# Seven block products in three accumulator banks instead of four

## The chip, the cores and the metric

The kernel runs on one core of one Trainium2 chip. The metric is the device time of one execution in microseconds (us). Before the change it is 582.73 us, the median of three runs (582.6 to 583.14).

## What is computed

A banded attention (two batches, eight heads, 768 positions of 64 numbers) is followed by two feed-forward blocks. The change touches the second one alone:

```python
def _moe2_ref(x, w_in, w_out):
    h = x @ w_in                                            # 1536 x 512 by 512 x 2048
    g = np.maximum(h, 0.0) + np.log1p(np.exp(-np.abs(h)))   # softplus
    return (g @ w_out).astype(np.float32)
```

Inputs are float32. The kernel keeps float32 accuracy by splitting each operand in a high and a low part, and making three matmuls of each product (`mm3`, lines 167 to 169).

## The kernel before

The last stage (`stage4`) computes this second block. It goes over three blocks t of 512 tokens, and in each over 16 slices f of 128 hidden columns. A slice is a bank `h` of 128 hidden columns by 512 tokens, made by 12 matmuls of 512 columns; ScalarE (ACT) and VectorE (DVE) turn it into softplus, split in `gh` and `gl`; and 12 more matmuls (`outs`) multiply these with the output weights, into four banks (`ox` and `o`, 128 tokens by 512 each) that stay open over all 16 slices. TensorE makes the `outs` of one slice while ACT and DVE work on the next.

Five pairs of slices (p = 2, 4, 6 in block 1, and p = 3, 5 in block 2) are made another way, by the function `seven`. The two slices of a pair, 256 hidden columns by 512 tokens, are seen as 2 x 2 blocks, as are the weights and the tokens, and are made of seven products of blocks instead of eight (the Strassen-Winograd scheme). The function `product` makes one block product: six matmuls of 256 columns, into one half (256 of 512 columns) of an accumulator bank. The sums of weights (`ws`, from `wr`) and of tokens (`ts`) that this needs are made by DVE and ACT ahead of the pair; the products are put together by DVE (`combine`, line 759) into `he` and `ho`, the two halves of the buffer `hp`, from which softplus goes on as for any other slice.

The banks of `h` and of the pairs come from one ring of four banks (tag "S"). A new buffer takes the bank of the one four places before it, and is written when that one's readers are done. In `seven` the four banks A, Bk, C and E are this whole ring:

- A, first half: product 1, copied out by ACT as `p1`; product 6 is later added to it.
- Bk, both halves: products 2 and 3.
- C, first half: product 4, then read once by DVE, for the sum `u3`.
- E, first half: product 5, which DVE adds to `u3`; product 7 is later added to it.

In this text the products have the numbers of the order in which they are made. Between them stand the `outs` of the slices before, written out by hand: three matmuls between products 3 and 4, nine between 5 and 6, three between 6 and 7, and nine behind 7. Blocks 1 and 2 are under a manual schedule: each engine runs its instructions in the order of the program. Waits between engines are set by the framework, which goes by tiles in accumulator memory.

Of the kernel before, what the change touches and what calls it, by code (L numbers as in the profile page):

```python
# [9 lines left out]
F32 = mybir.dt.float32  # L10
# [6 lines left out]
ALU = mybir.AluOpType  # L17
# [3 lines left out]
P = 128  # L21
B, H, S, D = 2, 8, 768, 64
# [17 lines left out]
CH = 512  # L40
NCH = NT // CH
HN, HM = slice(0, CH // 2), slice(CH // 2, CH)
# [17 lines left out]
    C=(-143.56, -520.69, 38.35, -348.75, -150.48, -361.46), T=(85.26, 85.11, 83.1, 84.82, 88.43, 82.09),  # L60
    P=(-697.11, -455.77, -631.6, -474.64, -647.58, -395.71), PV=(97.88, 94.31, 94.22, 97.88, 97.88, 169.98),
# [81 lines left out]
class Net:  # L143
# [581 lines left out]
    def stage4(self, pool, psum):  # L725
# [3 lines left out]
        def outs(t, f, g, parts=range(CH // P)):  # L729
            if f == 0:  # L730
                acc[t] = [psum.tile([P, CH], F32, tag=f"X{i}", name=f"ox{t}_{i}", bufs=1) for i in range(2)]
                acc[t] += [psum.tile([P, CH], F32, tag="PT", name=f"o{t}_{i}", bufs=2) for i in range(2)]
            wh, wl = self.w4[f]
            for i in parts:
                k = slice(i * P, (i + 1) * P)
                self.mm3(acc[t][i], (g[0][:, k], g[1][:, k]), (wh[:, 1, :], wl[:, 1, :]), f == 0, f == NF2 - 1)
# [21 lines left out]
        def combine(out, x, y, op):  # L758
            nc.vector.tensor_tensor(out=out, in0=x, in1=y, op=op)
# [49 lines left out]
        def product(ps, a, b, start=True):  # L809
            for c in range(2):  # L810
                self.mm3(ps, a(c), b(c), start and c == 0, c == 1, skip_group_check=True)

        def seven(t, p, before, todo):
            odd, even, x = self.w4[2 * p + 1], self.w4[2 * p], self.x2[t]

            def part(pair, c0):
                return lambda c: tuple(w[:, 0, (c0 + c) * P : (c0 + c + 1) * P] for w in pair)

            def tok(c0, cols):
                return lambda c: tuple(x[c0 + c][:, j, cols] for j in range(2))  # L820

            def wsum(j, c0):
                return lambda c: tuple(self.ws[j][:, k, (c0 + c) * P : (c0 + c + 1) * P] for k in range(2))

            def tsum(j, cols):
                return lambda c: tuple(self.ts[c, j][:, k, cols] for k in range(2))

            def quarter(tag, n):
                return self.dec.tile([P, CH // 2], F32, tag=tag, name=f"{n}_{t}_{p}", bufs=2)

            A, Bk, C, E = [psum.tile([P, CH], F32, tag="S", name=f"q{t}_{p}_{j}", bufs=4) for j in range(4)]
            h = self.slot(SLOT_X + 2, f"hp{t}_{p}", F32)
            he, ho = h[:, 0, :], h[:, 1, :]
            product(A[:, HN], part(odd, 0), tok(0, HN))
            p1 = quarter("dt", "p1")
            nc.scalar.copy(p1, A[:, HN])
            product(Bk[:, HN], part(even, 2), tsum(1, HN))
            product(Bk[:, HM], wsum(0, 0), tsum(1, HM))
            u2 = quarter("dc", "u2")
            combine(u2, Bk[:, HM], p1, ALU.add)  # L840
            outs(*todo[0], parts=[0])
            product(C[:, HN], wsum(1, 0), tsum(0, HM))
            u3 = quarter("dt", "u3")
            combine(u3, C[:, HN], u2, ALU.add)
            combine(he[:, HN], u3, Bk[:, HN], ALU.subtract)
            product(E[:, HN], wsum(1, 2), tsum(0, HN))
            combine(he[:, HM], E[:, HN], u3, ALU.add)
            before()
            outs(*todo[0], parts=[1, 2, 3])
            product(A[:, HN], part(odd, 2), tok(2, HN), False)  # L850
            outs(*todo[1], parts=[0])
            product(E[:, HN], wsum(0, 2), tok(2, HM), False)
            outs(*todo[1], parts=[1, 2, 3])
            e = self.softplus(pool, he, 2 * p, t)
            next(e)
            next(e)
            nc.scalar.copy(ho[:, HN], A[:, HN])
            combine(ho[:, HM], E[:, HN], u2, ALU.add)
            g = next(e)
            o = self.softplus(pool, ho, 2 * p + 1, t)  # L860
            next(o)
            next(steps.get((t, 2 * p + 1), (iter(lambda: 0, 1), ()))[0])
            next(o)
            return [(t, 2 * p, g)], (t, 2 * p + 1, o)
# [17 lines left out]
        for t in range(NCH):  # L882
            pairs = lots.get(t, ())
            with tc.manual_schedule() if t else contextlib.nullcontext():
                for f in range(NF2):
# [4 lines left out]
                    if f // 2 in pairs:  # L890
                        if f % 2 == 0:
                            def before():
                                todo.append((*last[:2], next(last[2])))

                            todo, last = seven(t, f // 2, before, todo)
                        continue
# [222 lines left out]
```

## Time and profile before

| | us |
|---|---|
| median of three runs | 582.73 |
| the profiled execution | 585.09 |
| its span, first to last instruction | 583.2 |
| TensorE busy | 573.7 |
| VectorE busy | 470.5 |
| ScalarE busy | 394.0 |

The profiled execution is 1.9 us longer than its span and 2.4 us longer than the median. In the tables of the profile PE is TensorE's matmuls, PEld its loads of weights (which run beside the matmuls before them), and the name behind "<-" in a wait is what ended it. A matmul's duration in these tables is longer than the distance to the next: they are pipelined, and the distance is what counts.

### The profile page before, as it was taken

The numbers are of one execution on the slowest core, as the hardware profiler recorded it, in microseconds if no ns is written. First come the engines' busy times: TensorE is split into PE (matmuls) and PEld (weight loads), VectorE is DVE, ScalarE is ACT, GpSimd is POOL, SyncE is SP. The second block draws the span as 40 slices with busy tenths as digits, with TensorE's granted clock in tenths as the row PEclk, the third lists the DMA queues.
The fourth block names the chain that finished last, engine by engine and source line by source line (L and its number), as shares of the span: only waits on it lengthen the run. The fifth ranks groups of instructions, "written<-read, shape, count | busy, mean of one in ns | idle before, by whom it ended". The sixth has DMA issues, their size and how long they took to land.

```text
span 583.2 us, 10109 instructions
## 1 busy us (share of the span) xinstructions
PE 573.7 (98%) x3808; PEld 476.0 (82%) x3808; DVE 470.5 (81%) x1004; ACT 394.0 (68%) x790; POOL 46.6 (8%) x113
## 2 busy tenths in 40 slices
PE   9999999999999999999999999999999999999995
PEld 7887788888788788888888788888888888888884
DVE  6889899999889976776998899965877867877663
ACT  6999967676566664554667989666665766666662
POOL 3757710000000000000000000000000000000000
PEclk9999999999999999999999999999999999999999
DMA  7666644444443632441744131000200000100002
GB/s 252 193 199 216 185 146 145 144 143 147 145 144 111 179 110 72 145 144 38 201 130 138 31 115 37 0 1 0 74 0 1 1 0 1 72 1 1 1 1 78
DMA packets 15514, 54.53 MB, mean 94 GB/s; under 512 B 1888, under 2 KB 1888, under 8 KB 15456
## 3 DMA queue, kind: packets, MB, share of 16 engines
q1 hardware_dynamic: 15312, 53.53, 30.0%
q8 instruction: 32, 0.52, 0.4%
q10 hardware_dynamic: 144, 0.26, 0.1%
q14 instruction: 26, 0.21, 0.1%
HBM read 50.64 MB, written 3.15 MB: 92 GB/s over the span
## 4 chain that ended last, share of the span: by engine, by line
PE 56%; DVE 9%; ACT 5%; DMA 4%; issue 1%; ACTq 0%; SPq 0%; DVEq 0%
PE h L168 5%; PE h L169 5%; PE h L167 5%; PE x2p L169 4%; PE x2p L167 4%; PE x2p L168 4%; PE ox L167 3%; PE ox L169 3%; PE o L168 3%; PE o L167 3%; PE o L169 3%; PE ox L168 3%; DMA raw_w<-w3t 3%; PE ab L169 3%; PE ab L167 3%; PE ab L168 3%
## 5 line engine op out<-in xcount | busy, mean ns | idle before, releaser
L194 ACT ACTIVATE dt_w<-raw_w 128x512 bf16<-128x512 bf16 x64 | 42.5, 670 | 53.5 <-DMA raw_w<-w4d 14.7
L167 PE MATMUL ab<-x,u_w 128*128 128x512 f32 x192 | 75.0, 391 | 0.3 <-ACT u_w L227 0.3
L169 PE MATMUL ab<-x,u_w 128*128 128x512 f32 x192 | 74.9, 390 | 0.3 <-DVE u_w L152 0.3
L168 PE MATMUL ab<-x,u_w 128*128 128x512 f32 x192 | 74.7, 389 | 0.0
L167 PE MATMUL h<-y,w4h 128*128 128x512 f32 x152 | 59.1, 389 | 0.0
L168 PE MATMUL h<-y,w4h 128*128 128x512 f32 x152 | 59.1, 389 | 0.0
L169 PE MATMUL h<-y,w4l 128*128 128x512 f32 x152 | 59.1, 389 | 0.0
L712 DVE SCALAR_TENSOR_TENSOR spu<-spu,spa 128x512 f32<-128x512 f32 (+1 forms) x49 | 33.2, 677 | 27.1 <-ACT spl L710 27.1
L202 DVE SCALAR_TENSOR_TENSOR dc_w<-raw_w,dt_w 128x512 uint16<-128x512 uint16 x64 | 44.2, 698 | 10.1 <-ACT dt_w L197 9.2
L721 ACT CAST gh<-spl 128x512 fp32r<-128x512 f32 x47 | 28.8, 614 | 29.9 <-DVE spl L718 29.9
L152 DVE TENSOR_TENSOR gl<-spl,gh 128x512 fp32r<-128x512 f32 x47 | 32.3, 688 | 19.6 <-ACT gh L721 19.4
L705 ACT ACTIVATE spa<-h 128x512 f32<-128x512 f32 (+1 forms) x39 | 22.8, 583 | 36.5 <-PE h L169 36.5
L197 ACT ACTIVATE dt_w<-dt_w,rebias 128x512 uint16<-128x512 uint16 x64 | 45.8, 722 | 1.3
L394 ACT ACTIVATE e<-e,st 128x196 f32<-128x196 f32 (+1 forms) x96 | 42.2, 447 | 1.5 <-DVE st L387 1.3
L169 PEld LDWEIGHTS ab<-x,u_w 128*128 128x128 f32 x192 | 36.0, 188 | 8.6 <-DVE u_w L152 1.2
L167 PEld LDWEIGHTS ab<-x,u_w 128*128 128x128 f32 x192 | 36.0, 188 | 8.4 <-ACT u_w L227 1.0
L168 PEld LDWEIGHTS ab<-x,u_w 128*128 128x128 f32 x192 | 36.0, 188 | 7.5
L408 POOL TENSOR_SCALAR e<-e,st 128x196 f32<-128x196 f32 (+1 forms) x96 | 39.7, 438 | 24.1 <-ACT e L394 16.9
L167 PE MATMUL x2p<-ab,w 128*128 128x512 f32 x96 | 37.3, 389 | 0.0
L168 PE MATMUL x2p<-ab,w 128*128 128x512 f32 x96 | 37.3, 389 | 0.0
L169 PE MATMUL x2p<-ab,w 128*128 128x512 f32 x96 | 37.3, 389 | 0.0
L167 PE MATMUL ox<-w4h,gh 128*128 128x512 f32 x94 | 37.0, 394 | 0.0
(172 smaller groups left out, 1449.6 us busy)
## 6 DMA issues: line engine op xcount, KB each, us to landing
raw_w<-w4d SPq DMA_DIRECT2D x32, 511.8 KB, 3.9
raw_w<-w SPq DMA_DIRECT2D x16, 511.8 KB, 4.7
raw_w<-w3t SPq DMA_DIRECT2D x16, 511.8 KB, 3.8
qk<-qk SPq DMA_DIRECT2D x7, 792.0 KB, 4.7
raw_wo<-wod SPq DMA_DIRECT2D x8, 511.8 KB, 3.7
v<-vu SPq DMA_DIRECT2D x8, 400.0 KB, 5.8
v<-v SPq DMA_DIRECT2D x8, 384.0 KB, 4.8
out<-os SPq DMA_DIRECT2D x11, 256.0 KB, 2.5
```

The costliest lines, as they stand in the source:

```text
L152: return engine.tensor_tensor(out=lo, in0=x, in1=hi.bitcast(F32), op=ALU.subtract)
L167: nc.tensor.matmul(ps, lhs[0], rhs[0], start=start, stop=False, **kw)
L168: nc.tensor.matmul(ps, lhs[0], rhs[1], start=False, stop=False, **kw)
L169: nc.tensor.matmul(ps, lhs[1], rhs[0], start=False, stop=stop, **kw)
L194: return nc.scalar.activation(t.bitcast(BF), x["top"].bitcast(BF), AF.Abs)
L197: return nc.scalar.activation(x["t"], x["t"], AF.Relu, bias=self.rebias[:, 0:1], scale=8.0)
L202: nc.vector.scalar_tensor_tensor(out=c, in0=x["top"], scalar=0x8000, in1=t, op0=ALU.bitwise_and, op1=ALU.bitwise_or)
L394: nc.scalar.activation(e, e, AF.Exp, bias=st[:, 0, i : i + 1], scale=-1.0, accum_out=st[:, 1, i : i + 1])
L408: nc.gpsimd.tensor_scalar(out=e, in0=e, scalar1=buf("st", h)[:, 2, i : i + 1], scalar2=1.0, op0=ALU.mult, op1=ALU.mult)
L705: nc.scalar.activation(a[:, c], ps[:, c], AF.Abs)
L712: nc.vector.scalar_tensor_tensor(out=u[:, c], in0=u[:, c], scalar=1.0, in1=a[:, c], op0=ALU.subtract, op1=ALU.subtract)
L721: self.last_hi = nc.scalar.copy(gh[:, c], l[:, c])
```

## The change

Bank E is gone. Products 5 and 7 are put into the second half of C, so that a pair takes three banks of the ring. The order of the instructions stays as it was on every engine.

```diff
-            A, Bk, C, E = [psum.tile([P, CH], F32, tag="S", name=f"q{t}_{p}_{j}", bufs=4) for j in range(4)]
+            A, Bk, C = [psum.tile([P, CH], F32, tag="S", name=f"q{t}_{p}_{j}", bufs=4) for j in range(3)]
...
             u3 = quarter("dt", "u3")
             combine(u3, C[:, HN], u2, ALU.add)
             combine(he[:, HN], u3, Bk[:, HN], ALU.subtract)
-            product(E[:, HN], wsum(1, 2), tsum(0, HN))
-            combine(he[:, HM], E[:, HN], u3, ALU.add)
+            product(C[:, HM], wsum(1, 2), tsum(0, HN))
+            combine(he[:, HM], C[:, HM], u3, ALU.add)
...
-            product(E[:, HN], wsum(0, 2), tok(2, HM), False)
+            product(C[:, HM], wsum(0, 2), tok(2, HM), False)
...
-            combine(ho[:, HM], E[:, HN], u2, ALU.add)
+            combine(ho[:, HM], C[:, HM], u2, ALU.add)
```

TensorE's rows at the end of product 4 and the start of product 5 in the first pair (block 1, p = 2), before the change. The buffers `q1_2_0` to `q1_2_3` are A, Bk, C and E; `ws` and `ts` are sums of weights and of tokens.

```order
L167 MATMUL q1_2_2_4682<-ts1_0_0_4378,ws1_2_1_4657 128x256
...
L169 MATMUL q1_2_2_4682<-ts1_1_0_4511,ws1_2_1_4657 128x256
L167 MATMUL q1_2_3_4683<-ts1_0_0_4378,ws1_2_1_4657 128x256 [waits DVE_49]
L168 MATMUL q1_2_3_4683<-ts1_0_0_4378,ws1_2_1_4657 128x256
...
L169 MATMUL q1_2_3_4683<-ts1_1_0_4511,ws1_2_1_4657 128x256
L167 MATMUL ox1_1_4616<-w4h2_3337,gh1_2_4604 128x512
```

The same place after the change.

```order
L167 MATMUL q1_2_2_4682<-ts1_0_0_4378,ws1_2_1_4657 128x256
...
L169 MATMUL q1_2_2_4682<-ts1_1_0_4511,ws1_2_1_4657 128x256
L167 MATMUL q1_2_2_4682<-ts1_0_0_4378,ws1_2_1_4657 128x256 [waits DVE_49]
L168 MATMUL q1_2_2_4682<-ts1_0_0_4378,ws1_2_1_4657 128x256
...
L169 MATMUL q1_2_2_4682<-ts1_1_0_4511,ws1_2_1_4657 128x256
L167 MATMUL ox1_1_4616<-w4h2_3337,gh1_2_4604 128x512
```

Nothing moved, and a wait for DVE stands at the same matmul; the buffer written is now that of product 4.

DVE's rows at this place after the change (before, the last of them read `q1_2_3`).

```order
L715 SCALAR_TENSOR_TENSOR spu1_3_4649<-h1_3_4631,spu1_3_4649 128x512 [waits DVE_49]
L718 TENSOR_TENSOR spl1_3_4650<-spl1_3_4650,spu1_3_4649 128x512 [waits DVE_49]
L759 TENSOR_TENSOR u2_1_2_4704<-q1_2_1_4681,p1_1_2_4690 128x256 [waits PE_49,Activation_49]
L759 TENSOR_TENSOR u3_1_2_4715<-q1_2_2_4682,u2_1_2_4704 128x256 [waits DVE_49,PE_49]
L759 TENSOR_TENSOR hp1_2_4683<-u3_1_2_4715,q1_2_1_4681 128x256 [waits DVE_49]
L759 TENSOR_TENSOR hp1_2_4683<-q1_2_2_4682,u3_1_2_4715 128x256 [waits PE_49]
```

DVE's order is that of before too. Its first reader of C is `u3`, in the fourth row.

## Rows read from the trace of the kernel before

**Rows 1.** Page, part 1: busy time of each engine.

```profile
PE 573.7 (98%) x3808; PEld 476.0 (82%) x3808; DVE 470.5 (81%) x1004; ACT 394.0 (68%) x790; POOL 46.6 (8%) x113
```

**Rows 2.** Busy time by stretch: length, busy us (instructions) by engine, clock, DMA.

```profile
419.00:570.00 151.00, 150.89 (x760) 128.17 (x759) 111.12 (x190) 99.09 (x173) 0.00 (x0) 1.00 0.02 8
```

**Rows 3.** Waits of PEld, 415 to 560 us: sum, times, longest.

```profile
PEld q L167 <- DVE spu L715: 0.7, 3, 0.3
```

**Rows 4.** Timeline, first pair, PE: last `h` matmul, then product 5.

```profile
416.98 0.39 PE L169 MATMUL h<-y,w4l 128*128 128x512 f32 x1
...
423.48 0.28 PE L167 MATMUL q<-ts,ws 128*128 128x256 f32 x1
423.60 0.28 PE L168 MATMUL q<-ts,ws 128*128 128x256 f32 x1
...
424.08 0.28 PE L169 MATMUL q<-ts,ws 128*128 128x256 f32 x1
```

**Rows 5.** Timeline, first pair, DVE: `u3`, and the sum with product 5.

```profile
424.35 0.42 DVE L759 TENSOR_TENSOR u<-q,u 128x256 f32<-128x256 f32 x1
...
425.15 0.42 DVE L759 TENSOR_TENSOR hp<-q,u 128x256 f32<-128x256 f32 x1
```

**Rows 6.** One tile (`u`): `u3` in all pairs, ns min/median/max, first and last start.

```profile
L759 DVE TENSOR_TENSOR u<-q,u x5: 425/425/425, 424.3 to 543.9; 128x256 f32<-128x256 f32 x5
```

**Rows 7.** Timeline, second pair: last `h` matmul, L715, product 5, `u3`.

```profile
438.39 0.39 PE L169 MATMUL h<-y,w4l 128*128 128x512 f32 x1
...
444.31 0.69 DVE L715 SCALAR_TENSOR_TENSOR spu<-h,spu 128x512 f32<-128x512 f32 x1
...
445.05 0.19 PEld L167 LDWEIGHTS q<-ts,ws 128*128 128x128 f32 x1 [0.20 <-DVE spu L715]
...
445.06 0.39 PE L167 MATMUL q<-ts,ws 128*128 128x256 f32 x1
...
445.28 0.28 PE L168 MATMUL q<-ts,ws 128*128 128x256 f32 x1
...
446.17 0.42 DVE L759 TENSOR_TENSOR u<-q,u 128x256 f32<-128x256 f32 x1
```

**Rows 8.** Timeline, pairs 3 to 5: last `h` matmul, product 5's second matmul, `u3`.

```profile
460.06 0.39 PE L169 MATMUL h<-y,w4l 128*128 128x512 f32 x1
...
467.09 0.28 PE L168 MATMUL q<-ts,ws 128*128 128x256 f32 x1
...
467.98 0.42 DVE L759 TENSOR_TENSOR u<-q,u 128x256 f32<-128x256 f32 x1
...
514.70 0.39 PE L169 MATMUL h<-y,w4l 128*128 128x512 f32 x1
...
521.32 0.28 PE L168 MATMUL q<-ts,ws 128*128 128x256 f32 x1
...
522.07 0.42 DVE L759 TENSOR_TENSOR u<-q,u 128x256 f32<-128x256 f32 x1
...
536.11 0.39 PE L169 MATMUL h<-y,w4l 128*128 128x512 f32 x1
...
543.00 0.28 PE L168 MATMUL q<-ts,ws 128*128 128x256 f32 x1
...
543.89 0.42 DVE L759 TENSOR_TENSOR u<-q,u 128x256 f32<-128x256 f32 x1
```

**Rows 9.** Waits of ACT, 415 to 560 us: sum, times, longest.

```profile
ACT ws L774 <- DVE wr L759: 1.0, 3, 0.4
```

**Rows 10.** The end: last matmul, and the clock after it (as in rows 2).

```profile
576.97 0.39 PE L169 MATMUL o<-w4h,glast 128*128 128x512 f32 x1
...
580.00:581.00 1.00, 0.00 (x0) 0.00 (x0) 0.00 (x0) 0.00 (x0) 0.00 (x0) 0.72 0.13 39
581.00:582.00 1.00, 0.00 (x0) 0.00 (x0) 0.00 (x0) 0.00 (x0) 0.00 (x0) 0.50 0.03 10
```

## The prediction

> **What bounds the kernel now.** The page's first part comes first: TensorE is busy for 573.7 us, 98% of the span, VectorE for 81% and ScalarE for 68% [rows 1]. Over the whole stretch that holds the five pairs the table by stretches gives TensorE 150.89 of 151.00 us at the full granted clock [rows 2]. So TensorE sets the time there, and no slice waits for anything. Whatever holds TensorE up in a pair goes to the end one for one, since no later idle time could take it in; work moved on VectorE or ScalarE costs nothing as long as TensorE doesn't wait for it. The waits of TensorE come next, and they are few: in this stretch product 5 waited three times for line 715 of VectorE, 0.7 us in all [rows 3]. That line is the last reader of `h` in the slice before the pair, and E takes that slice's bank. Last comes the order of times within a pair: when TensorE reaches product 5, and when VectorE makes `u3`.
>
> **What the change removes.** The wait for line 715. It bit in pairs 2, 3 and 5. Its price is read from the distance between the slice's last matmul and the second matmul of product 5 (the second, because a stalled first matmul has its own distance to the next): 423.60 - 416.98 = 6.62 us in pair 1 [rows 4], 445.28 - 438.39 = 6.89 in pair 2 [rows 7], and by the same reading 7.03, 6.62 and 6.89 in pairs 3, 4 and 5 [rows 8]. 6.62 is the distance without a stall, so the stalls cost 0.27, 0.41 and 0.27, in sum 0.95 us.
>
> Instructions removed: none. Matmuls, sums and copies are the same in number, size and order on each engine, and no DMA moves, so SP's and POOL's queues are as before. Those terms are zero, and nothing has to hide them.
>
> **What it adds.** The first matmul of product 5 now writes C, and it still carries a wait for VectorE. What VectorE has to do with C before this point is `u3`, which reads product 4 from the other half of the bank. A wait for that reader is the only one that the new place calls for: C's own place in the ring was freed by the slice two before the pair. So product 5, which stood right behind product 4, now stands behind product 4 and `u3`. Nothing lies between them on TensorE, and behind product 5 are queued the nine `outs` matmuls, product 6 and all the rest.
>
> When would `u3` be done? In pair 1 it starts at 424.35 [rows 5] and takes 0.425 us in every pair [rows 6], so it ends at 424.775, while TensorE begins product 5 at 423.48 [rows 4]. VectorE is not kept by TensorE here: `u3` follows `u2`, which follows the softplus of the slice before. Its times come from that slice's last matmul, through ScalarE and VectorE: 424.35 - 416.98 = 7.37 us in pair 1, 446.17 - 438.39 = 7.78 in pair 2 [rows 7], then 7.92, 7.37 and 7.78 [rows 8].
>
> How long from VectorE's end to TensorE in full flow? That is shown by the wait of today, which has the same form: line 715 ends at 444.31 + 0.69 = 445.00, the load of weights starts at 445.05 and the second matmul at 445.28 [rows 7]. So 0.28 us.
>
> In each pair the second matmul of product 5 would then be at (distance to `u3`) + 0.425 + 0.28 behind the slice's last matmul:
>
> - with the distances to `u3` as they are: 8.075, 8.485, 8.625, 8.075, 8.485; less today's 6.62, 6.89, 7.03, 6.62, 6.89 this is 1.455 + 1.595 + 1.595 + 1.455 + 1.595 = 7.70 us;
> - with 7.37 in every pair: 5 x 8.075 - 34.05 = 6.33 us.
>
> **Which of the two.** Pairs 2, 3 and 5 follow closely on another pair, and their extra 0.41, 0.55 and 0.41 us before `u3` have a visible source: ScalarE, ready to cast `ws`, waited for VectorE's sums `wr`, three times and 1.0 us in all [rows 9]. VectorE was behind with work left from the pair before. After the change TensorE is later by 1.455 us from pair 1 on, and so is the slice from which pair 2's times are counted. VectorE's leftover work is later by less. Its sum with product 5 ran at 425.15 [rows 5]; now product 5's last matmul starts at 424.08 + 1.455 and ends 0.28 later [rows 4], at 425.82, so this sum and what follows are some 0.67 us later. Against TensorE, VectorE and ScalarE thus gain about 0.79 us between the pairs (part of which ScalarE loses again, as it then waits for the next slice). The extra 0.41 to 0.55 should be gone. I take the second sum: **+6.3 us**. The distance of 7.37 can't shrink further by a lead, since it is work that starts only at the slice's last matmul, as pairs 1 and 4 show, which came after slices without leftovers.
>
> What is late next: the softplus of `he`, by 0.67 us, against a TensorE that is later by 1.455; so its `outs` don't wait. The slices after the pair take older banks than before, and carry no wait that they did not have.
>
> **A rule weighed.** In rows 7 the load of weights for the waiting matmul doesn't start before the wait ends, and the two matmuls are 0.22 us apart, where they are 0.12 apart in full flow [rows 4]; this is in the 0.28 above. The Trainium skill (TensorE: Matmul & The Clock Gate, the step on LDWEIGHTS in Part 2) says that TensorE's queue pulls a load of weights ahead of matmuls in flight. By that the load would be done during the wait. The restart would be 0.05 + 0.12 = 0.17 instead of 0.28, and the sum 5 x 7.965 - 34.05 = 5.78 us. The row has the load held back too, so I go by the row.
>
> **The sum.** 585.09 + 6.33 = 591.4 us against the profiled execution. That one lies 2.36 us above the median, so the median goes from 582.73 to **589.0 us**, 1.1% slower.
>
> **Rivals.**
>
> 1. *No lead.* VectorE stays as far behind in pairs 2, 3 and 5 as today: +7.70, 590.4 us. For it: the leftovers are longest there. Against it: the 0.79 us worked out above. 15%.
> 2. *Weights loaded during the wait.* +5.78, 588.5 us. For it: loads run ahead of matmuls everywhere else in the trace. Against: rows 7. 5%. This is what the skill's rule would make of it.
> 3. *The clock falls.* Each pair leaves TensorE idle for about 1.3 us. At the end of the program the granted clock is down to 0.72 at 580 to 581 us and to 0.50, the lower level of 1.2 GHz, from 581 [rows 10]; the last matmul ended at 577.36, so 2.6 us of idleness went by without a fall. That speaks against it. If it did fall, and stayed down for as long as those 2.6 us, a stretch that does half its work would cost 1.3 us more in each pair: 589.0 + 6.5 = 595.5 us. 4%.
> 4. *Not slower.* The wait in product 5 is not one for `u3` but for something older, because the halves of a bank are followed apart. Place: the first matmul of product 5. Price: with nothing to wait for all five distances are 6.62, and 0.95 us comes back: 581.8 us, no measurable change. It decides from the point where the awaited instruction ends within 423.48 - 416.98 = 6.50 us of the slice's last matmul; `u3` ends 7.37 + 0.425 = 7.80 after it, 1.3 us too late, so this needs another instruction. Line 715, for one, would do in pairs 1 and 4. Against it: no other instruction of VectorE's touches C, the wait stands in the order, and without any need it would not. This is also the case that the change does nothing but free a bank. 2%.
>
> **Numbers.** The forecast has 72%, the rivals 15, 5, 4 and 2, and 2% is left for what I don't see. The range takes in the forecast and rivals 1 and 2, from 588.5 to 590.4, and 0.4 us on each side for the spread of the runs (582.6 to 583.14): **588.1 to 590.8**. A measurement of this kernel tells 0.2% (1.2 us) from no change. Beyond that: slower 0.97, with rivals 1 to 3 and most of the unseen; same 0.02, rival 4; faster 0.01.
>
> **What the profile after would show.** Right: among TensorE's waits one of product 5 for VectorE's line 759, five times, about 1.2 us of idle matmul time each, 6 in all, and none for line 715; the second matmul of product 5 some 8.08 us behind the slice's last matmul in every pair; ScalarE's wait for `wr` gone or much smaller; the stretch of the pairs longer by 6.3 us with the same busy time, the clock full; all before 419 us unchanged. Wrong: distances of 8.5 in pairs 2, 3 and 5 (rival 1); a load of weights that starts before `u3` ends (rival 2); a clock under full behind a pair (rival 3); no wait at product 5 (rival 4). A wait at another place, as of a slice's `outs` for `gh`, would mean that I overlooked a chain.

## The result, and the profile after

The changed kernel takes 589.01 us (median of six runs, 588.28 to 590.68), the kernel before 582.93 us (six runs, 582.26 to 583.44). The ratio is 1.0102, with a 95% interval of 1.0086 to 1.0118. Forecast were 589.0 us and 1.1% slower.

The profiled execution took 589.42 us. First the page of the changed kernel, part 1, to be held against [rows 1]:

```profile
PE 573.3 (98%) x3808; PEld 475.8 (81%) x3808; DVE 470.9 (80%) x1004; ACT 393.0 (67%) x790; POOL 46.4 (8%) x113
```

The same work on each engine, and still 98% for TensorE: the page's first part doesn't show a change of this size. The waits do. Those of the weight loads (PEld) in the changed kernel from 415 to 570 us (sum, times, longest):

```profile
PEld q L167 <- DVE u L759: 7.0, 5, 1.4
PEld ox L167 <- DVE os L750: 0.3, 1, 0.3
```

And those of the matmuls (PE) in the same stretch, a list of one line:

```profile
PE q L167 <- DVE u L759: 5.9, 5, 1.2
```

The wait for line 715 [rows 3] is gone, and in its place stands one for line 759, the sum `u3`, in each of the five pairs. The timelines of the changed kernel show it where [rows 4, 5, 7, 8] showed the kernel before. The first pair:

```profile
415.71 0.39 PE L169 MATMUL h<-y,w4l 128*128 128x512 f32 x1
...
423.08 0.42 DVE L759 TENSOR_TENSOR u<-q,u 128x256 f32<-128x256 f32 x1
...
423.56 0.19 PEld L167 LDWEIGHTS q<-ts,ws 128*128 128x128 f32 x1 [1.39 <-DVE u L759]
...
423.56 0.39 PE L167 MATMUL q<-ts,ws 128*128 128x256 f32 x1 [1.18 <-DVE u L759]
423.79 0.28 PE L168 MATMUL q<-ts,ws 128*128 128x256 f32 x1
```

The other four pairs:

```profile
438.57 0.39 PE L169 MATMUL h<-y,w4l 128*128 128x512 f32 x1
...
445.95 0.42 DVE L759 TENSOR_TENSOR u<-q,u 128x256 f32<-128x256 f32 x1
...
446.65 0.28 PE L168 MATMUL q<-ts,ws 128*128 128x256 f32 x1
...
461.44 0.39 PE L169 MATMUL h<-y,w4l 128*128 128x512 f32 x1
...
468.81 0.42 DVE L759 TENSOR_TENSOR u<-q,u 128x256 f32<-128x256 f32 x1
...
469.51 0.28 PE L168 MATMUL q<-ts,ws 128*128 128x256 f32 x1
...
517.08 0.39 PE L169 MATMUL h<-y,w4l 128*128 128x512 f32 x1
...
524.46 0.42 DVE L759 TENSOR_TENSOR u<-q,u 128x256 f32<-128x256 f32 x1
...
525.16 0.28 PE L168 MATMUL q<-ts,ws 128*128 128x256 f32 x1
...
539.92 0.39 PE L169 MATMUL h<-y,w4l 128*128 128x512 f32 x1
...
547.30 0.42 DVE L759 TENSOR_TENSOR u<-q,u 128x256 f32<-128x256 f32 x1
...
548.00 0.28 PE L168 MATMUL q<-ts,ws 128*128 128x256 f32 x1
```

Subtract each pair's first row from the others. `u3` stands 7.37 or 7.38 us behind the slice's last matmul in all five pairs, where it was 7.37 to 7.92 before, and product 5's second matmul 8.07 or 8.08 us, where it was 6.62 to 7.03. From the slice before pair 1 to product 5 of pair 5 the two kernels compare so, in the table by stretches (columns as in [rows 2]), before and after:

```profile
416.98:543.00 126.02, 125.91 (x643) 107.18 (x641) 96.86 (x169) 81.83 (x140) 0.00 (x0) 1.00 0.03 9
```

```profile
415.71:548.00 132.29, 126.36 (x642) 107.41 (x641) 98.67 (x172) 81.91 (x141) 0.00 (x0) 1.00 0.02 9
```

The stretch is 6.27 us longer with TensorE's busy time within 0.5 us and the full clock. The two profiled spans differ by less, 587.6 to 583.2, which is 4.4 us: in this execution the unchanged part ahead of the pairs was 1.27 us shorter (415.71 to 416.98), and the part from the last matmul on, with the stores, 0.6 us. No run shows why these two parts differ. The medians are 6.1 us apart.

### The profile page after: what moved, and what is told of

It is laid out like the page before. It is cut to its first block, busy times and chain, and to the rows that moved or that the text cites. A ratio compares the mean times of both kernels' runs of the same rounds, so it can differ in the third digit from the quotient of the medians.

```text
span 587.6 us, 10109 instructions
## 1 busy us (share of the span) xinstructions
PE 573.3 (98%) x3808; PEld 475.8 (81%) x3808; DVE 470.9 (80%) x1004; ACT 393.0 (67%) x790; POOL 46.4 (8%) x113
## 4 chain that ended last, share of the span: by engine, by line
PE 59%; DVE 8%; ACT 4%; DMA 4%; issue 2%; DVEq 0%; SPq 0%; ACTq 0%
PE h L169 6%; PE h L168 6%; PE h L167 6%; PE x2p L168 4%; PE x2p L167 4%; PE x2p L169 4%; PE o L167 3%; PE o L169 3%; PE o L168 3%; PE ox L167 3%; PE ox L169 3%; PE ox L168 3%; PE ab L169 3%; PE ab L168 3%; PE ab L167 3%; DMA raw_w<-w3t 2%
```

## The experiments

The theory to be tested: TensorE stands still at product 5 until `u3`, which comes a fixed time after the slice before; only this wait costs, not the number of banks, nor the sharing of one; and the stall lets VectorE make good its lag. The rivals stand with each run. Each experiment is timed against runs of the kernel before on the same chip: 583.02 us (seven runs) for the doubled sum and for the two kernels with nine matmuls inside the wait, 583.31 us (18 runs) for the other four.

**Three banks, without the wait.** Products 5 and 7 go into the other half of A. Product 5 no longer carries the flag that starts a sum (the last argument, `False`): of the products in A only product 1 has it.

```diff
-            product(C[:, HM], wsum(1, 2), tsum(0, HN))
-            combine(he[:, HM], C[:, HM], u3, ALU.add)
+            product(A[:, HM], wsum(1, 2), tsum(0, HN), False)
+            combine(he[:, HM], A[:, HM], u3, ALU.add)
...
-            product(C[:, HM], wsum(0, 2), tok(2, HM), False)
+            product(A[:, HM], wsum(0, 2), tok(2, HM), False)
...
-            combine(ho[:, HM], C[:, HM], u2, ALU.add)
+            combine(ho[:, HM], A[:, HM], u2, ALU.add)
```

> Three banks, but products 5 and 7 go into the second half of A, whose first half ScalarE copied out some 1.6 us before, instead of C. My theory (the cost is the wait for u3, and nothing in the sharing of a bank or in three banks as such): no wait at product 5, the stalls for line 715 gone too, since C's bank was freed by an older slice. All five distances from the slice's last matmul to product 5's second are 6.62 us, 0.95 us less than before in sum. Product 6 now waits for the sum of he with product 5, which ends some 9.0 to 9.2 us behind the slice's last matmul in pairs 2, 3 and 5, about where product 6 starts (9.3, its load earlier), so up to 0.3 us comes back. Time 582.0 to 582.3 against 582.9. Rival (a bank that holds two open products, or a ring with three taken banks, costs by itself): near 589, or between.

Measured: 582.58 us, ratio 0.9987 (0.9975 to 1.0). The waits of this kernel's weight loads, 412 to 570 us:

```profile
PEld ox L169 <- DVE gl L152: 0.4, 1, 0.4
PEld ox L167 <- DVE os L750: 0.3, 1, 0.3
```

No wait at product 5 is left. Its second matmul is 6.63, 6.63, 6.89, 6.62 and 6.62 us behind the slices, in sum 0.66 us less than before; the medians differ by 0.73. The 0.26 us that came back in pair 3 are the wait for `gl` in the list, which ends at 463.57 us, ahead of product 4, and not that of product 6 for the sum of `he`, which I had expected. So a pair with three banks, and with products 5 and 7 in a bank beside others, costs nothing here. What cost 6 us was which bank they share.

**Four banks taken, the wait left in.**

```diff
-            A, Bk, C = [psum.tile([P, CH], F32, tag="S", name=f"q{t}_{p}_{j}", bufs=4) for j in range(3)]
+            A, Bk, C, _ = [psum.tile([P, CH], F32, tag="S", name=f"q{t}_{p}_{j}", bufs=4) for j in range(4)]
```

> The changed kernel, but a pair still takes four banks of the ring, the fourth unused. My theory: the wait for u3 stands as it is, the number of banks is of no account, 589.0 us, five stalls of about 1.2 us at product 5, distances 8.08. Rival (the cost or a part of it comes from the other banks that slices and pairs now get): clearly off 589, towards 583.

Measured: 589.07 us, ratio 1.0097 (1.0072 to 1.0121). The waits of its weight loads, 412 to 570 us:

```profile
PEld q L167 <- DVE u L759: 6.9, 5, 1.4
PEld ox L167 <- DVE os L750: 0.3, 1, 0.3
```

As the theory has it: the wait and the time are those of the changed kernel. The number of banks that a pair takes from the ring is of no account here.

**Three matmuls of other work inside the wait.**

```diff
-            product(C[:, HM], wsum(1, 2), tsum(0, HN))
+            outs(*todo[0], parts=[1])
+            product(C[:, HM], wsum(1, 2), tsum(0, HN))
             combine(he[:, HM], C[:, HM], u3, ALU.add)
             before()
-            outs(*todo[0], parts=[1, 2, 3])
+            outs(*todo[0], parts=[2, 3])
```

> The changed kernel with three of the nine outs matmuls moved from behind product 5 to between products 4 and 5: 0.70 us of work inside the wait. Theory with the lead (TensorE's stalls let VectorE catch up before the next pair): stalls of 8.075 - 7.32 = 0.76 us in pairs 1 and 4; the sum of he is as late as in the changed kernel, TensorE 0.70 less, so hardly any lead is left, u3 in pairs 2, 3 and 5 stays near 7.75 to 7.9 us behind the slice, and stalls there are about 1.1 to 1.25. In sum 5.0 of stalls against today's 0.95: 587.0 us. Rival (stalls are the same in each pair, and 0.70 is taken off each): 589.0 - 3.5 = 585.5 us, with u3 at 7.37 in every pair.

Measured: 586.84 us, ratio 1.0055 (1.0036 to 1.0075). `u3` is at 7.38, 7.71, 7.73, 7.38 and 7.71 us behind the slices. Pair 2, with the slice's last matmul, `u3` and product 5's second matmul:

```profile
437.28 0.39 PE L169 MATMUL h<-y,w4l 128*128 128x512 f32 x1
...
444.99 0.42 DVE L759 TENSOR_TENSOR u<-q,u 128x256 f32<-128x256 f32 x1
...
445.70 0.28 PE L168 MATMUL q<-ts,ws 128*128 128x256 f32 x1
```

The two kinds of pair differ again, as they did before the change, and ScalarE's wait behind the lag is back (its waits in this kernel, 412 to 570 us; in the changed kernel this line is absent):

```profile
ACT ws L774 <- DVE wr L759: 0.7, 3, 0.2
```

The time is that of the theory with the lead (587.0), 1.3 us above its rival's; `u3` in pairs 2, 3 and 5 comes just ahead of the 7.75 to 7.9 us expected, and far from the rival's 7.37. A stall of 1.46 us gives VectorE the time to make its lag good; one of 0.76 doesn't.

**One more sum ahead of `u3`.**

```diff
             combine(u2, Bk[:, HM], p1, ALU.add)
+            combine(u2, Bk[:, HM], p1, ALU.add)
```

> The changed kernel with the sum u2 made twice on VectorE, ahead of u3: one more sum of 256 columns in each pair, which at the pitch of today's u2 and u3 (0.52 us from start to start) puts u3 about 0.45 to 0.55 us later. My theory (TensorE stands still until u3, and nothing gives it back): product 5's second matmul 8.5 to 8.6 us behind the slice's last matmul in all five pairs, 2.3 to 2.7 us more in sum, 591.3 to 591.7 us. Rival (VectorE has room, as it is idle for a fifth of the span): 589 us.

Measured: 591.16 us, ratio 1.0144 (1.0127 to 1.016). `u3` is at 7.83 or 7.84 us and product 5's second matmul at 8.54 in all pairs, 0.46 later than in the changed kernel. Pair 1:

```profile
414.91 0.39 PE L169 MATMUL h<-y,w4l 128*128 128x512 f32 x1
...
422.74 0.42 DVE L759 TENSOR_TENSOR u<-q,u 128x256 f32<-128x256 f32 x1
...
423.45 0.28 PE L168 MATMUL q<-ts,ws 128*128 128x256 f32 x1
```

In sum this is 5 x 0.46 = 2.3 us. The median is 2.15 us above that of the changed kernel, or 2.06 when each is taken against its own runs of the kernel before; it lies just under the forecast 591.3. VectorE's idle fifth lies elsewhere: the sum put ahead of `u3` shows in the time at about its full 0.46 us per pair.

**`u3` ahead of the softplus.** The last softplus steps of the slice before are held back and made behind `u3` and the first sum of `he`.

```diff
             combine(he[:, HN], u3, Bk[:, HN], ALU.subtract)
+            next(late)
             product(C[:, HM], wsum(1, 2), tsum(0, HN))
...
-                    next(sp)
+                    if (f + 1) // 2 not in pairs or f % 2 == 0:
+                        next(sp)
                     last = (t, f, sp)
```

(`late` is the softplus of the slice before; two more lines, not shown, hand it to `seven`.)

> The changed kernel with the last softplus steps of the slice before (lines 710 to 718) moved on ScalarE and VectorE from ahead of u2 and u3 to behind u3 and the first sum of he. My theory (u3 is late because VectorE does the softplus first, not because product 4 is late): u3 starts right behind product 4, about 6.7 us behind the slice's last matmul instead of 7.37, and product 5's second matmul is at 7.43 instead of 8.08. Stalls of 0.81 us in five pairs, 4.05 in sum: 586.0 us, up to 586.8 where the later softplus holds up other matmuls. Rival (u3 waits for product 4 or for TensorE's order): u3 stays at 7.37, 589 us.

Measured: 588.51 us, ratio 1.0081 (1.0057 to 1.0104). The time was missed (forecast were 586.0 to 586.8 us), and the mechanism came out in two pairs of five. In pairs 1 and 4 `u3` is at 6.71 us and product 5 at 7.41, as forecast: VectorE now waits for product 4 there.

```profile
422.60 0.42 DVE L759 TENSOR_TENSOR u<-q,u 128x256 f32<-128x256 f32 x1 [0.91 <-PE q L169]
```

In pairs 2, 3 and 5 `u3` is at 7.38 or 7.39 all the same, but not for the reason it has in the changed kernel: here too it waits for product 4, which is late. Pair 2:

```profile
445.46 0.42 DVE L759 TENSOR_TENSOR u<-q,u 128x256 f32<-128x256 f32 x1 [0.97 <-PE q L169]
```

The later softplus put VectorE behind, and TensorE waits for its `ws` and `gl` ahead of product 4 (waits of this kernel's weight loads, 412 to 570 us):

```profile
PEld q L167 <- DVE u L759: 3.6, 5, 0.7
PEld ox L169 <- DVE gl L152: 1.9, 4, 0.6
PEld q L169 <- DVE ws L152: 1.1, 3, 0.4
```

**The wait covered in full, with three banks and with four.** Nine matmuls go between products 4 and 5, first in the changed kernel, then in the kernel before.

```diff
+            outs(*todo[0], parts=[1, 2, 3])
             product(C[:, HM], wsum(1, 2), tsum(0, HN))
             combine(he[:, HM], C[:, HM], u3, ALU.add)
             before()
-            outs(*todo[0], parts=[1, 2, 3])
```

> The changed kernel with all nine outs matmuls moved from behind product 5 to between products 4 and 5 (2.04 us of work inside the wait). In pairs 1 and 4 the wait for u3 is covered: no stall at product 5, whose second matmul comes some 8.7 us behind the slice's last. But the sum of he, and all softplus behind it, comes 1.3 us later than before the change, while TensorE isn't later, so VectorE is behind in pairs 2, 3 and 5: u3 at some 9.0 to 9.4 us there, stalls of about 1 us at product 5 and small ones at ws and gl. Time 584 to 587 us. Rival (covering the wait ends the cost, a lead or lag is of no account): 582 us, no stalls in any pair.

```diff
+            outs(*todo[0], parts=[1, 2, 3])
             product(E[:, HN], wsum(1, 2), tsum(0, HN))
             combine(he[:, HM], E[:, HN], u3, ALU.add)
             before()
-            outs(*todo[0], parts=[1, 2, 3])
```

> The kernel before, with four banks, in the same new order: nine outs matmuls between products 4 and 5. No wait for u3 is there, and line 715 has long ended. VectorE is behind in pairs 2, 3 and 5 as in the kernel with three banks and this order, so what is left are the small stalls at ws and gl: 582.5 to 584.5 us. The difference to that kernel is the wait for u3 in pairs 2, 3 and 5 alone. Rival (the new order by itself costs as much): the same time as that kernel, within 0.5 us.

Measured: 586.88 us, ratio 1.0066 (1.005 to 1.0083), and 587.01 us, ratio 1.0071 (1.0054 to 1.0088). The two are the same, so the rival of the second run holds, and its forecast of 582.5 to 584.5 us was missed: the new order costs by itself, and the wait for `u3` costs nothing there. The waits of the weight loads, 412 to 570 us, first with three banks, then with four:

```profile
PEld ox L169 <- DVE gl L152: 4.1, 9, 1.0
PEld q L169 <- DVE ws L152: 1.3, 3, 0.4
PEld q L167 <- ACT ws L774: 0.6, 3, 0.2
PEld ox L167 <- DVE os L750: 0.3, 1, 0.3
```

```profile
PEld ox L169 <- DVE gl L152: 4.1, 9, 1.0
PEld q L169 <- DVE ws L152: 1.3, 3, 0.4
PEld q L167 <- ACT ws L774: 0.6, 3, 0.2
PEld ox L167 <- DVE os L750: 0.3, 1, 0.3
```

No line for `u3` in either. With three banks it comes 8.91 to 8.93 us behind the slice in pairs 2, 3 and 5, a little ahead of the 9.0 to 9.4 that I had worked out. But TensorE had by then been held up by 1 us for `ws` and `gl` of the same late VectorE, and product 5 came after `u3` by itself. I had put these stalls down as small, and the loss at product 5; that the first run's time fell within its 584 to 587 us was luck. VectorE's rows show where the stalls begin, here with three banks in pair 1, whose slice ended at 415.00:

```profile
424.49 0.42 DVE L759 TENSOR_TENSOR hp<-q,u 128x256 f32<-128x256 f32 x1 [1.23 <-PE q L169]
424.83 0.68 DVE L152 TENSOR_TENSOR gl<-spl,gh 128x512 fp32r<-128x512 f32 x1
```

The sum of `he` waits for product 5, and `gl` of the slice before stands behind that sum in VectorE's order. The `outs` behind product 6 need this `gl`, and the softplus of `he` is late as well. With the nine matmuls behind product 5, as in the kernel before, the sum starts 8.17 us behind the slice instead of 9.49.

## Why the prediction was right

*TensorE sets the time, and a stall in a pair goes to the end one for one.* Shown: from product 5 of pair 5 to the last matmul (576.97 before, 581.97 after) both kernels take 33.97 us. The doubled sum bears it out, with 2.06 to 2.15 us between the medians for 2.3 in the pairs.

*The new wait is one for `u3`.* Shown by the lists of waits. That it follows from the bank is shown by the run with A's second half, in which it is absent. Whether products in separate halves of a bank could go on beside VectorE's read of the other half wasn't tried, as that would mean taking away the wait itself.

*7.37 us + 0.425 + 0.28 in each pair.* Measured 8.07 to 8.08 for 8.075. The restart of 0.28 us, taken from stalls of 0.2 us, holds for stalls of 1.2 us too: in pair 1 423.79 - (423.08 + 0.42) = 0.29. The load of the waiting matmul started at 423.56, only as the wait ended (`u3` ends at 423.50), as in the row that the forecast rested on [rows 7], and rival 2 falls. The Trainium skill (TensorE: Matmul & The Clock Gate, Part 2) says that, on conditions that it names, weight loads are pulled ahead of matmuls in flight. The trace doesn't show it for a matmul that waits: in all five pairs the load starts 0.05 to 0.06 us after `u3` ends.

*The lead.* It chose 6.33 over 7.70. The sum with product 5 starts 8.87 us behind the slice in pair 1, where it was 8.17: 0.70 us later, for the 0.67 worked out, against 1.46 for TensorE. The changed kernel's five equal distances and the missing wait for `wr` [rows 9] show the lead. The run with three matmuls inside the wait takes the lead away, and the lag is there again. Rival 1 falls.

*The clock.* 1.00 over the whole stretch of pairs, with five stalls of 1.2 us. Rival 3 falls.

*The 0.95 us of the old wait.* The trace of the bank A run has no wait for line 715, and product 5 is 0.66 us earlier in sum, with 0.26 lost to another wait. As a gain in time this isn't shown: the medians are 0.73 us apart, and the interval of the ratio reaches up to 1.0.

*What came out otherwise.* All before 419 us was to be unchanged; in the profiled execution it was 1.27 us shorter, and that execution took 589.42 us, not 591.4. That the median met 589.0 to 0.01 us is partly luck: its six runs spread over 2.4 us, and the difference of the medians is 6.08 us for 6.33.

## What to carry to other kernels

In this kernel, where the framework sets the waits by tiles in accumulator memory, the second of two products that share a bank waited for the reader of the first, though it read the other half. So look up when that reader runs, not only whether the bank has room. The bank whose content had been copied out took the next product at no cost; the one whose reader was still queued cost that reader's lateness: here the same saving of one bank cost 6 us in one bank and nothing in another. Where the bounding engine waits at a fixed distance behind an earlier step, measure that distance per occurrence; pairs that differ today may become alike, as the stall itself gives the lagging engine time.

## What was not expected

Moving 2 us of matmuls ahead of product 5 made the kernel 0.7% slower than the kernel before with either number of banks, although it covers the wait in full. The order of the matmuls that seem to be mere filling decides when the next engine starts, and here that start had no slack: with a sum of `he` 1.3 us later in pair 1, and more in pairs 2, 3 and 5, the weight loads waited 4.1 us for `gl` (412 to 570 us), where it was 0.2 us before the change.
